# Attention and two MoE layers on one core: the first batch in two query pieces, weights converted 512 columns wide, and moved priorities in the instruction planner

## The chip, the cores and the metric

One Trainium2 chip, one of its NeuronCores. The time is the device time of one execution in microseconds (us). The engines are PE (TensorE; PEld is its weight load), DVE (VectorE), ACT (ScalarE), POOL (GpSimd) and SP (SyncE, which issues nearly all DMAs here).

## The reference

The inputs are q, k, v of shape (4, 8, 576, 64) in float32, a threshold tau, and float64 weights. Three steps follow each other:

```python
scores = scale * np.matmul(q, k.transpose(0, 1, 3, 2))
thresh = np.max(scores, axis=-1, keepdims=True) - tau
scores = np.where(scores >= thresh, scores, -1000000000.0)
attn = softmax(scores);  x = np.matmul(attn, v)         # to (2304, 512)
h = x @ w_in                                            # 512 to 1024
solu = h * softmax(h);  x = (layer_norm(solu) * g_ln) @ w_out
h = x @ w2_in                                           # 512 to 2048
out = (h * np.tanh(softplus(h))) @ w2_out
```

## The kernel before

**How the instructions are ordered.** The kernel does not issue its instructions as the Python code reads. Each step is recorded as a task with an engine, a planned duration, what it depends on, and which buffer slots it takes and uses (`add`). `Plan.run` (L261) then plays the whole list forward: `forward` (L135) gives each engine, whenever it is free, the ready task with the highest key, and returns the order with planned begin and end times; `backward` (L207) plays it from the end and so sets new keys. After 40 turns of this, with six settings each, the order with the shortest planned length is issued. Every engine runs its instructions in that order; so does SP's queue with its DMAs. A slot of a ring of buffers is free for its next taker when the last users are done.

**Attention.** The 32 heads go in 16 pairs, four pairs to each of the four batches. Queries are cut in five tiles: four of 128, and a fifth that holds the last 64 queries of both heads. For each pair `operands` (L593) loads K and Q of both heads (one load of Q each, in two cuts for the first pair) and `load_v` V. For each tile and head `s_tile` (L617) computes a score tile of 128x576 on PE (L640 in the first eight pairs, L649 in the others), takes the row maximum on DVE (L655), the exp on ACT (L656) and the threshold with row sum on DVE (L659): nine score tiles for a pair. For the first four pairs every third tile uses a third score bank, `s3`. `turn` (L669) transposes the result on PE (L684, L687) and copies it out of PSUM on ACT. At the last tile of a pair it also takes the reciprocals of the nine row sums (L677, L678), writes them to a DRAM tensor `rd` and reads them back spread over partitions, in four DMAs. `pv` (L723) multiplies with V (L732), once for the first 256 queries and once for the other 320; after the second, POOL scales all 576 columns (L746) and one DMA writes them to `xd`.

**First MoE.** `x_split` (L761) loads a tile of 128 tokens from `xd`, waiting for all four pairs of the batch, and splits it in a high and a low word (L772, L773). `moe_h` multiplies with W1 (L784), `layer_norm` follows, `moe_t` transposes, and `moe_y` multiplies with W2 (L854).

**Conversions.** `convert` (L474) turns a block of float64 weights of 128 rows by CW = 256 columns into float32: a DMA to `cr`; on ACT the low words (L491) and, for W1 and W2, the absolute high words (L497); on DVE a mask for the second MoE's weights (L494), then clamp (L499), shift (L500) and merge (L502); on POOL the sum (L507 or L509). W1 and W2 then get a high and a low word each (L521, L522). The rings are four slots of `cr` and two each of `cz`, `cl` and `cf`. W1 takes 16 such blocks, W2 16, and the weights of the second MoE 64, 96 in all. The latter are put together in `ws`, seven blocks of a Strassen product with four DVE operations (L555), and go to DRAM as `w2c`.

**Second MoE.** `ff_in` and `ff_out` multiply with the seven products of Strassen's scheme (PE, L948), and fetch the weights from `w2c` with `load_w`. The loop that records the attention's tasks is

```python
for p in range(NH // 2 + 1):
    if p < NH // 2:
        operands(2 * p); operands(2 * p + 1); load_v(p)
    for i in range(QT):
        ...            # s_tile, turn for each head
        if p and i == 0:
            pv(p - 1, 1)
        if p < NH // 2 and i == 2:
            pv(p, 0)
```

Of the kernel before, what the change touches and what calls it, by code (L numbers as in the profile page):

```python
# [8 lines left out]
F32 = mybir.dt.float32  # L9
# [7 lines left out]
TABLES = {n: list(get_activation_tables("")).index(s) for n, s in (("exp", "natural_log_exp_and_others"), ("mish", "mish"))}  # L17

# [40 lines left out]
class Plan:  # L59
# [73 lines left out]
    ORDER = {e: k for k, e in enumerate(("PE", "DVE", "ACT", "POOL", "SP", "-"))}  # L133

# [126 lines left out]
    def run(self):  # L261
# [50 lines left out]
def kernel(  # L312
# [30 lines left out]
    CW = 256  # L343
    PN = 256
    NP = NT // PN
    M0 = 4
    TU = 3 * PN
# [42 lines left out]
    rd = [dram.tile([2 * QT - 1, 128], F32, name=f"rd{i}") for i in range(NH // 2)]  # L390
# [77 lines left out]

    b_cr = buf("cv", "cr", [128, CW, WN], U32 if WN == 2 else F32, 4)
    b_cz = buf("cv", "cz", [128, CW], U32, 2)  # L470
    b_cl = buf("cv", "cl", [128, CW], U32, 2)
    b_cf = buf("cv", "cf", [128, CW], U32, 2)

    def convert(src, r0, c0, put, gain=None, into=None):  # L474
        cr = b_cr.new()
        if into and c0[1] - c0[0] > 128:
            fetch = lambda: D(cr.tile.rearrange("p (i a) b -> p i (a b)", i=2),
                              src[r0:r0 + 128].rearrange("p (i a) -> p i a", i=2)[:, :, c0[0] * WN:(c0[0] + 128) * WN])
        else:
            first = c0[0] if into else c0  # L480
            fetch = lambda: D(cr.tile.rearrange("p a b -> p (a b)"), src[r0:r0 + 128, first * WN:(first + CW) * WN])
        t_f = add("SP", dma(128 * CW * 4 * WN), fetch, new=[cr])
        if WN == 1:
            x, t = lambda: cr.tile[:, :, 0], t_f
            slots = [cr]
        else:
# [17 lines left out]
            if into:  # L504
                at, n, slots, order = into
                wide = lambda x: x.tile.rearrange("p (a b) -> p a b", a=n)
                return add("POOL", gps(CW), lambda: G.tensor_tensor(at(), wide(cf), wide(cl), ALU.add), [t4, t2],  # L507
                           slots if order is None else [], [cl, cf, *slots], order=[order])
            t = add("POOL", gps(CW), lambda: G.tensor_tensor(cf.tile, cf.tile, cl.tile, ALU.add), [t4, t2], use=[cl, cf])  # L509
            slots = [cf]  # L510
        if into:
            at, n, slots, order = into
            return add("DVE", dve(CW), lambda: V.tensor_scalar(f(at()), x().rearrange("p (a b) -> p a b", a=n), 1.0, None, ALU.mult), [t],
                       slots if order is None else [], [cr, *slots], order=[order], port=True)
# [31 lines left out]
    for g in range(NQ):  # L546
        for x, src in enumerate((w2_in, w2_out)):
            WST[x, g] = []
            for k in range(2):
                ws, wh, ts = b_ws.new(), b_wh.new() if x not in RAW else None, []  # L550
                for j in range(2):
                    at = lambda ws=ws, j=j: ws.tile.bitcast(U32)[:, j:7:4 + j]
                    row, cols = ((2 * j + k) * 128, (g * 256, g * 256 + 128)) if x == 0 else ((2 * g + j) * 128, (k * 128, 256 + k * 128))
                    ts.append(convert(src, row, cols, None, into=(at, 2, [ws], ts[0] if ts else None)))
                add7 = lambda o, a, b, op, ws=ws: (dve(128), lambda: V.tensor_tensor(*(f(ws.tile[:, z]) for z in (o, a, b)), op))  # L555
                t = chain("DVE", [add7(3, 4, 6, ALU.add), add7(2, 3, 0, ALU.subtract), add7(5, 1, 2, ALU.subtract), add7(4, 0, 4, ALU.subtract)], ts, use=[ws], port=True)
# [21 lines left out]
    RX, OPS, VL, E, EX, EVT, XST = ({} for _ in range(7))  # L578
# [14 lines left out]
    def operands(n):  # L593
        if n < 2 * R0:
# [3 lines left out]
            for z, c in enumerate((slice(0, 256), slice(256, SP)) if n < 2 else (slice(0, SP),)):  # L598
                w = c.stop - c.start
                q = add("SP", dma(512 * w), lambda c=c: D(f(qh.tile[:, c]), qq[n // H_, n % H_][:, c]), [], [qh] * (z == 0), [qh], order=OPS[n][0][1:])  # L600
                eng, e, cost = (V, "DVE", dve2(w)) if n < 2 else (G, "POOL", 0.16 + w * 0.95e-3)
# [15 lines left out]
    def s_tile(p, i, h):  # L617

        third = p < M0 and (9 * p + 2 * i + h) % 3 == 2
        st, m = (b_s3 if third else b_st).new(), b_m.new()  # L620
        if i == h == 0:
            RX[p] = [b_sr.new()]
# [20 lines left out]
        def go():  # L643
            for c, w in ((0, 256), (256, KW)):
                for y, n in enumerate(heads):
                    _, ks, qh, ql = OPS[n]
# [6 lines left out]
                [t for n in heads for t in OPS[n][0][:2 if p == 0 and i < 2 else None]], [st], slots, mode=int(p < R0))  # L653
# [69 lines left out]
    def pv(p, c):  # L723
# [10 lines left out]
        if c == 0:  # L734
            EVT[p] = [b_xo.new()]
# [425 lines left out]
```

## Time and profile before

| | |
|---|---|
| median of 3 runs | 889.31 us (885.67 to 889.76) |
| profiled execution | 889.64 us, of which the trace spans 887.9 |
| PE, DVE busy | 846.4 and 781.9 us |
| ACT, POOL busy | 617.1 and 338.4 us |
| moved by DMA | 192.6 MB, 217 GB/s over the span |

A profile shows one execution. A group's line gives line, engine and operation, the tiles (out<-in), the count, and behind the bar busy us and mean ns of one, then how long the engine sat idle before it and what ended that. Matmuls are pipelined: one that is shown as 336 ns may follow its forerunner after half of that, so PE can show itself busy at less than its pace. PEclk is the granted clock as a share of full speed.

### The profile page before, as it was taken

The page shows a single profiled execution, that of the slowest core. Times are in us where ns is not written, and L with a number is a line of the kernel's source. Part 1 is how long each engine was busy: PE and PEld are TensorE (multiplying, and loading weights), DVE is VectorE, ACT ScalarE, POOL GpSimd, SP SyncE. Part 2 cuts the span into 40 slices and gives each one's busy share as a digit, 9 for nine tenths or more (in the row PEclk, how much of TensorE's full clock was granted, in tenths as well). Part 3 has the DMA queues.
Part 4 walks back from the last instruction along what each step waited for, and adds up shares of the span by engine and source line. Part 5 has one row for each costly group of instructions (what it writes and reads, how often), then busy time and mean ns, then how long its engine had stood idle before and what let it go on. Part 6 is the DMA issues. An engine that isn't in the chain of part 4 may idle for free.

```text
span 887.9 us, 16722 instructions
## 1 busy us (share of the span) xinstructions
PE 846.4 (95%) x5419; PEld 736.5 (83%) x5419; DVE 781.9 (88%) x1808; ACT 617.1 (70%) x1368; POOL 338.4 (38%) x430
## 2 busy tenths in 40 slices
PE   8898999999999999999999999999999999999997
PEld 4555666777797888887788898999989999999997
DVE  7999889888988999898868899999999997788767
ACT  5888889868888879867555768665756664546432
POOL 2567776666674666444243221112212100010000
PEclk9999999999999999999999999999999999999999
DMA  5545543333746555454997499999999778788541
GB/s 180 187 158 162 170 143 104 121 113 100 228 132 213 166 175 161 130 183 146 324 382 220 143 308 309 386 333 359 328 371 302 250 216 277 231 273 281 191 152 72
DMA packets 154071, 192.62 MB, mean 217 GB/s; under 512 B 15088, under 2 KB 107776, under 8 KB 153984
## 3 DMA queue, kind: packets, MB, share of 16 engines
q1 hardware_dynamic: 153840, 191.55, 66.1%
q8 instruction: 43, 0.70, 0.3%
q14 instruction: 44, 0.36, 0.1%
q10 hardware_dynamic: 144, 0.00, 0.0%
HBM read 140.32 MB, written 51.19 MB: 216 GB/s over the span
## 4 chain that ended last, share of the span: by engine, by line
PE 49%; DVE 19%; ACT 9%; DMA 8%; issue 4%; POOL 3%; SPq 1%; POOLq 0%; DVEq 0%; ACTq 0%
PE hoa L948 21%; PE hob L948 7%; PE p_mo L784 4%; PE p_ta L732 4%; PE p_mo L854 4%; PE p_ta L684 3%; DMA B<-w2c 3%; DVE e L659 3%; PE st L649 2%; DVE m L655 2%; ACT e L656 2%; PE st L640 2%; DVE cf L502 2%; DVE gl L1033 1%; DMA w2c<-ws 1%
## 5 line engine op out<-in xcount | busy, mean ns | idle before, releaser
L948 PE MATMUL hoa<-y,A 128*128 128x384 f32 x648 | 125.7, 336 | 1.1 <-ACT gf L995 1.1
L948 PE MATMUL hoa<-gh,B 128*128 128x384 f32 x484 | 123.5, 336 | 1.2 <-DVE acc L1069 0.9
L659 DVE SCALAR_TENSOR_TENSOR e<-st,m,e 128x576 f32<-128x576 f32 x132 | 106.0, 813 | 15.2 <-ACT e L656 8.0
L948 PEld LDWEIGHTS hoa<-y,A 128*128 128x128 f32 x648 | 112.6, 188 | 2.7 <-ACT gf L995 2.6
L656 ACT ACTIVATE e<-st,m 128x576 f32<-128x576 f32 x132 | 97.0, 744 | 25.7 <-DVE m L655 25.0
L655 DVE TENSOR_REDUCE m<-st 128x1 f32<-128x576 f32 x132 | 97.3, 751 | 17.7 <-PE st L649 9.2
L1005 POOL TENSOR_TENSOR gf<-gf 128x384 f32<-128x384 f32 x24 | 27.6, 1152 | 214.2 <-DVE gf L1005 211.0
L507 POOL TENSOR_TENSOR ws<-cf,cl 128x256 uint32<-128x256 uint32 x64 | 61.1, 964 | 113.7 <-DMA w2c<-ws 59.9
L684 PE MATMUL p_ta<-ident,e 128*128 128x128 f32 x576 | 85.4, 277 | 9.0 <-ACT ey L667 3.0
L1033 DVE TENSOR_TENSOR gl<-gf,gh 128x384 fp32r<-128x384 f32 x168 | 88.9, 567 | 0.7 <-ACT gh L1031 0.7
L948 PEld LDWEIGHTS hoa<-gh,B 128*128 128x128 f32 x484 | 87.0, 188 | 2.8 <-DVE acc L1069 1.9
L684 PEld LDWEIGHTS p_ta<-ident,e 128*128 128x128 f32 x576 | 65.3, 140 | 28.1 <-ACT ey L667 5.9
L854 PE MATMUL p_mo<-LH,W2H 128*128 128x256 f32 x288 | 83.2, 289 | 0.8 <-ACT ys L867 0.8
L948 PE MATMUL hoa<-gl,B 128*128 128x384 f32 x242 | 81.0, 335 | 1.3 <-DVE gl L1033 1.3
L854 PE MATMUL p_mo<-LL,W2H 128*128 128x256 f32 x288 | 81.4, 283 | 0.0
L854 PE MATMUL p_mo<-LH,W2L 128*128 128x256 f32 x288 | 81.4, 283 | 0.0
L1031 ACT ACTIVATE gh<-gf 128x384 fp32r<-128x384 f32 x168 | 77.8, 515 | 0.5 <-DVE gf L1005 0.2
L658 POOL TENSOR_SCALAR m<-m,cs 128x1 f32<-128x1 f32 x144 | 48.4, 339 | 70.8 <-DVE m L655 58.6
L1001 ACT ACTIVATE gf<-gf 128x384 f32<-128x384 f32 x72 | 37.6, 524 | 45.9 <-DVE gf L998 45.3
L1069 DVE TENSOR_TENSOR acc<-acc,hoa 128x384 f32<-128x384 f32 x101 | 54.1, 547 | 14.7 <-PE hoa L948 12.8
L784 PE MATMUL p_mo<-W1H,XH 128*128 128x512 f32 x144 | 60.6, 421 | 2.8 <-DVE LL L839 2.8
L854 PEld LDWEIGHTS p_mo<-LH,W2H 128*128 128x128 f32 x288 | 55.0, 191 | 2.0 <-ACT ys L867 1.1
(127 smaller groups left out, 2299.1 us busy)
## 6 DMA issues: line engine op xcount, KB each, us to landing
A<-w2c SPq DMA_DIRECT2D x140, 256.0 KB, 4.4
y<-yc SPq DMA_DIRECT2D x28, 768.0 KB, 8.6
w2c<-ws SPq DMA_DIRECT2D x32, 448.0 KB, 4.6
B<-w2c SPq DMA_DIRECT2D x112, 128.0 KB, 4.0
cr<-w_in SPq DMA_DIRECT2D x48, 256.0 KB, 3.3
cr<-w_out SPq DMA_DIRECT2D x48, 256.0 KB, 3.5
yc<-yh SPq DMA_DIRECT2D x9, 896.0 KB, 7.0
yc<-ys SPq DMA_DIRECT2D x9, 896.0 KB, 5.3
```

The costliest lines, as they stand in the source:

```text
L507: return add("POOL", gps(CW), lambda: G.tensor_tensor(at(), wide(cf), wide(cl), ALU.add), [t4, t2], slots if order is None else [], [cl, c ...
L655: t = add("DVE", dve(S), lambda: V.tensor_reduce(m.tile[:, 2:3], x(), AX.XY, ALU.max, negate=True), [t], [m], [st])
L656: a = add("ACT", act(S, True) + 0.1, lambda: SC.activation(et(), x(), ACTF.Exp, bias=m.tile[:, 2:3]), [t], [e] if h == 0 else (), [st, m, ...
L658: b = add("POOL", 0.26, lambda: G.tensor_scalar(m.tile[:, 1:2], m.tile[:, 2:3], -1.0, nt8, ALU.mult, ALU.add), [t], use=[m])
L659: t = add("DVE", dve(S) + 0.06, lambda: V.scalar_tensor_tensor(et(), x(), m.tile[:, 1:2], et(), ALU.is_ge, ALU.mult, accum_out=sr.tile[:, ...
L684: TE.transpose(tp.tile[:, k * 128:(k + 1) * 128], e.tile[:, o:o + 128], ident)
L784: TE.matmul(h.tile, l.tile[:, kt], r[:, kt, j * 512:(j + 1) * 512], start=(kt == 0 and x == 0), stop=(kt == KD - 1 and x == 2))
L854: TE.matmul(y.tile[:, :PN], l[:, k, cs], r.tile[:, k], start=(k == 0 and x == 0), stop=(k == KF - 1 and x == 2))
L948: TE.matmul(x.tile[:, :TH], l, r, start=new and n == 0, stop=stop and n == len(steps) - 1, skip_group_check=True)
L1031: a = add("ACT", act(TH), lambda h=h, x=x: SC.activation(h.tile, full(x), ACTF.Copy), [first], [h], [h, x])
L1033: out[c] = h, l, add(e, cost(TH), lambda h=h, l=l, x=x, eng=eng: eng.tensor_tensor(l.tile, full(x), f(h.tile), ALU.subtract), [a, *deps], ...
L1069: d = add("DVE", dve(TH), lambda: V.tensor_tensor(to(), to(), fr(), ALU.add), deps + [CO.get((v, e, i, t))], use=[ac, x])
```

## The change

Three things change. First, the four pairs of the first batch (NS = 4) are recorded in two pieces: all four pairs with their first 256 queries (tiles 0 and 1), then all four with the other 320 (tiles 2 to 4). K, V and the piece's cut of Q are loaded for each piece anew; row sums, `rd`, the scaling and the write to `xd` are made for each piece; `x_split` waits only for the columns that it reads. The third score bank serves the first pieces alone, 5 tiles where it was 12. Second, CW is 512: half as many conversions, with one slot each of `cz`, `cl` and `cf` and two of `cr`. For the second MoE's weights two DMAs fill one `cr`, and the seven blocks of `ws` stand in another order (`SLOT`). Third, `Plan.run` takes the best order's setting and keys, moves the keys of stretches of that order by 568 recorded draws (`moved`), plays forward once more and issues that order.

```diff
+    def moved(self, order):
...
+            middle, half, rare = draw() % len(order), 20 + draw() % 400, 1 + draw() % 5
+            size = (1.0, 3.0, 10.0, 30.0)[draw() % 4]
+            for t in order[max(0, middle - half):middle + half]:
+                if draw() % (1 << rare) == 0:
+                    t.key -= size * (draw() % 2001 - 1000) / 500.0
...
-                    best = length, order, {x: x.bank for x in self.shared}
+                    best = length, order, (wait, avoid), [t.key for t in self.tasks]
             self.backward()
+        for t, t.key in zip(self.tasks, best[3]):
+            pass
+        self.moved(best[1])
+        order = self.forward(*best[2])
+        best = max(t.end for t in order), order, {x: x.bank for x in self.shared}
...
-    CW = 256
+    CW = 512
+    NS = 4
...
-    b_cr = buf("cv", "cr", [128, CW, WN], U32 if WN == 2 else F32, 4)
-    b_cz = buf("cv", "cz", [128, CW], U32, 2)
-    b_cl = buf("cv", "cl", [128, CW], U32, 2)
-    b_cf = buf("cv", "cf", [128, CW], U32, 2)
+    b_cr = buf("cv", "cr", [128, CW, WN], U32 if WN == 2 else F32, 2)
+    b_cz = buf("cv", "cz", [128, CW], U32, 1)
+    b_cl = buf("cv", "cl", [128, CW], U32, 1)
+    b_cf = buf("cv", "cf", [128, CW], U32, 1)
...
-        third = p < M0 and (9 * p + 2 * i + h) % 3 == 2
+        part = p < NS
+        third = p < M0 and ((4 * p + 2 * i + h) % 3 == 2 and i * 128 < C0 if part else (9 * p + 2 * i + h) % 3 == 2)
...
-        if c:
-            *r, rx = RX[p][-5:]
-            ts = [add("POOL", gps(S), lambda: G.tensor_tensor(xo.tile, xo.tile, rx.tile, ALU.mult), EVT[p][1:] + r, use=[xo, rx])]
+        if c or part:
+            if c == 0 or not part:
+                XST[p] = []
+            rx, r = RB[p]
+            o = cs if part else slice(0, S)
+            n = o.stop - o.start
+            t = add("POOL", gps(n), lambda: G.tensor_tensor(xo.tile[:, o], xo.tile[:, o], rx.tile[:, o], ALU.mult), EVT[p][1:] + r, use=[xo, rx])
             k = p % (H_ // 2) * 128
-            XST[p] = add("SP", dma(128 * S * 4), lambda: D(xd[p // (H_ // 2)][k:k + 128, :], xo.tile), ts, use=[xo])
+            XST[p].append((o, add("SP", dma(512 * n), lambda: D(xd[p // (H_ // 2)][k:k + 128, o], xo.tile[:, o]), [t], use=[xo])))
...
-                [XST[p] for p in range(b * H_ // 2, (b + 1) * H_ // 2)], [] if ld else [xr], [xr], ld[:1]))
+                [q for p in range(b * H_ // 2, (b + 1) * H_ // 2) for c, q in XST[p] if c.start < s + l and c.stop > s], [] if ld else [xr], [xr], ld[:1]))
...
-    for p in range(NH // 2 + 1):
-        if p < NH // 2:
-            operands(2 * p)
-            operands(2 * p + 1)
+    todo = []
+    for p, piece in [(p, z) for z in range(2) for p in range(NS)] + [(p, None) for p in range(NS, NH // 2)] + [(None, None)]:
+        if p is not None:
+            operands(2 * p, piece)
+            operands(2 * p + 1, piece)
             load_v(p)
-        for i in range(QT):
+        for i in (range(QT) if piece is None else range(2) if piece == 0 else range(2, QT)):
...
+            while todo:
+                pv(*todo.pop())
+            if p is not None and piece is None and i == 2:
                 pv(p, 0)
+        todo = [(p, piece if piece == 0 else 1)]
```

## Rows read from the trace of the kernel before

**Rows 1.** The page: busy time (part 1); last chain by engine (part 4)

```profile
PE 846.4 (95%) x5419; PEld 736.5 (83%) x5419; DVE 781.9 (88%) x1808; ACT 617.1 (70%) x1368; POOL 338.4 (38%) x430
...
PE 49%; DVE 19%; ACT 9%; DMA 8%; issue 4%; POOL 3%; SPq 1%; POOLq 0%; DVEq 0%; ACTq 0%
```

**Rows 2.** Stages: us; PE, PEld, DVE, ACT, POOL busy (count); PEclk, DMA, GB/s

```profile
0.00:104.00 104.00, 89.09 (x597) 54.46 (x598) 91.34 (x219) 84.81 (x196) 59.40 (x109) 1.00 0.54 172
104.00:440.00 336.00, 325.69 (x2277) 263.94 (x2276) 300.74 (x696) 269.93 (x569) 198.58 (x247) 1.00 0.52 160
440.00:540.00 100.00, 95.42 (x639) 87.85 (x638) 82.28 (x203) 64.39 (x133) 32.67 (x30) 1.00 0.82 267
540.00:888.00 348.00, 336.23 (x1912) 330.28 (x1910) 307.52 (x693) 197.97 (x474) 47.72 (x45) 1.00 0.80 271
```

**Rows 3.** Chain that ended last, in time: start us, us, what

```profile
84.88 5.07 PE p_ta L732 x40
...
494.73 5.72 PE p_mo L784 x24
...
572.30 9.36 PE hoa L948 x54
```

**Rows 4.** Timeline of PE: start us, us, engine, line, operation

```profile
77.04 1.09 PE L684 MATMUL p_ta<-ident,e 128*128 128x128 f32 x8
...
99.49 1.78 PE L640 MATMUL st<-Kst,Qhh 64*128 64x320 f32 x12
```

**Rows 5.** Windows of the first stage's two halves, columns as in 2

```profile
0.00:56.00 56.00, 46.26 (x300) 27.91 (x301) 47.62 (x116) 41.87 (x93) 26.25 (x53) 1.00 0.55 176
56.00:104.00 48.00, 42.83 (x298) 26.55 (x298) 43.72 (x103) 42.94 (x104) 33.14 (x56) 1.00 0.53 167
```

**Rows 6.** Window 56 to 104, PE alone: L640, then L684, then L732

```profile
56.00:104.00 48.00, 16.26 (x96) 1.00 0.53 167
...
56.00:104.00 48.00, 13.05 (x87) 1.00 0.53 167
...
56.00:104.00 48.00, 12.52 (x100) 1.00 0.53 167
```

**Rows 7.** Tile W1H; min/median/max ns, first and last start us

```profile
L784 PE MATMUL p_mo<-W1H,XH x144: 387/395/504, 104.2 to 499.6; 128*128 128x512 f32 x144
...
L522 POOL TENSOR_TENSOR W1L<-cf,W1H x16: 724/732/862, 22.7 to 87.4; 128x256 fp32r<-128x256 f32 x16
```

**Rows 8.** Timeline of POOL and ACT: pair four's scaling, first token tile's split

```profile
92.49 1.41 POOL L746 TENSOR_TENSOR xo<-xo,rx 128x576 f32<-128x576 f32 x1
...
100.27 0.63 ACT L772 ACTIVATE XH<-XR 128x512 fp32r<-128x512 f32 x1
```

**Rows 9.** Tile cr (min/median/max ns), then groups by line (busy us, mean ns)

```profile
L502 DVE SCALAR_TENSOR_TENSOR cf<-cr,cz x96: 355/417/1793, 20.2 to 701.4; 128x256 uint32<-128x256 uint32 x96
...
L499 DVE TENSOR_SCALAR cz<-cz 128x256 f32<-128x256 f32 x96 | 35.7, 379 | 2.2 <-ACT cz L497 2.1
...
L491 ACT ACTIVATE cl<-cr 128x256 uint32<-128x256 uint32 x96 | 41.0, 440 | 13.1 <-POOL ws L507 13.0
...
L507 POOL TENSOR_TENSOR ws<-cf,cl 128x256 uint32<-128x256 uint32 x64 | 61.1, 964 | 113.7 <-DMA w2c<-ws 59.9 <-DVE cf L502 29.4 <-DVE cz L500 6.8
```

**Rows 10.** Groups by line: wider operations of like kind on DVE, ACT, POOL

```profile
L539 DVE TENSOR_TENSOR ws<-ws,wh 128x896 fp32r<-128x896 f32 x16 | 18.2, 1136 | 1.0 <-ACT wh L538 1.0
...
L538 ACT ACTIVATE wh<-ws 128x896 fp32r<-128x896 f32 x16 | 15.2, 949 | 8.8 <-DVE ws L555 8.6 <-DMA B<-w2c 0.2
...
L773 POOL TENSOR_TENSOR XL<-XR,XH 128x512 fp32r<-128x512 f32 x18 | 23.3, 1294 | 24.8 <-ACT XH L772 14.8 <-DMA A<-w2c 6.4 <-ACT ln L810 3.4
```

**Rows 11.** Line L491 on ACT: idle before it (us, times), by ender

```profile
  POOL ws L507: 13.0, 10
```

**Rows 12.** Timeline of PE: the last matmul

```profile
883.62 0.34 PE L948 MATMUL hoa<-gl,B 128*128 128x384 f32 x1
```

**Rows 13.** Window 640 to 720, columns as in 2

```profile
640.00:720.00 80.00, 76.73 (x435) 74.70 (x434) 79.64 (x195) 49.94 (x121) 17.00 (x18) 1.00 0.91 295
```

More of the change, by code (lines that the diff above doesn't have):

```diff
@@ L389 @@
     xd = [dram.tile([DM, S], F32, name=f"xd{i}") for i in range(B)]
[L390 removed]
+    rd = [dram.tile([2 * QT - 1, 128], F32, name=f"rd{i}") for i in range(NH // 2 + NS)]
     P = {"cv": pools(ctx, side="right")("cv")}
@@ L504, in convert @@
             if into:
[L505 to L508, printed above, removed]
+                return add("POOL", gps(CW), lambda: G.tensor_tensor(into[1].tile[:, :4].rearrange("p (a j) n -> p j a n", j=2).bitcast(U32),
+                           *(x.tile.rearrange("p (j a n) -> p j a n", j=2, a=2) for x in (cf, cl)), ALU.add), [t4, t2],
+                           [into[1]], [cl, cf, into[1]])
             t = add("POOL", gps(CW), lambda: G.tensor_tensor(cf.tile, cf.tile, cl.tile, ALU.add), [t4, t2], use=[cl, cf])
@@ L511, in convert @@
         if into:
-            at, n, slots, order = into
-            return add("DVE", dve(CW), lambda: V.tensor_scalar(f(at()), x().rearrange("p (a b) -> p a b", a=n), 1.0, None, ALU.mult), [t],
-                       slots if order is None else [], [cr, *slots], order=[order], port=True)
+            return add("DVE", dve(CW), lambda: V.tensor_scalar(into[1].tile[:, :4].rearrange("p (a j) n -> p j a n", j=2).bitcast(F32),
+                       x().rearrange("p (j a n) -> p j a n", j=2, a=2), 1.0, None, ALU.mult), t_f, [into[1]], [cr, into[1]], port=True)
         if gain is not None:
@@ L549 @@
             for k in range(2):
[L550 to L554, printed above, removed]
+                ws, wh = b_ws.new(), b_wh.new() if x not in RAW else None
+                if x:
+                    part_of = lambda j, src=src, g=g, k=k: src[(2 * g + j) * 128:(2 * g + j + 1) * 128].rearrange(
+                        "p (a b) -> p a b", a=2)[:, :, k * 128 * WN:(k + 1) * 128 * WN]
+                else:
+                    part_of = lambda j, src=src, g=g, k=k: src[(2 * j + k) * 128:(2 * j + k + 1) * 128, g * 256 * WN:(g + 1) * 256 * WN]
+                t = convert(None, (0, 1 - x), None, None, into=(part_of, ws))
                 add7 = lambda o, a, b, op, ws=ws: (dve(128), lambda: V.tensor_tensor(*(f(ws.tile[:, z]) for z in (o, a, b)), op))
-                t = chain("DVE", [add7(3, 4, 6, ALU.add), add7(2, 3, 0, ALU.subtract), add7(5, 1, 2, ALU.subtract), add7(4, 0, 4, ALU.subtract)], ts, use=[ws], port=True)
+                t = chain("DVE", [add7(4, 2, 3, ALU.add), add7(5, 4, 0, ALU.subtract), add7(6, 1, 5, ALU.subtract), add7(2, 0, 2, ALU.subtract)], [t], use=[ws], port=True)
                 if x in RAW:
@@ L577 @@
     b_rx = buf("xs", "rx", [128, S])
-    RX, OPS, VL, E, EX, EVT, XST = ({} for _ in range(7))
+    RB, XST = {}, {}
+    RX, OPS, VL, E, EX, EVT = ({} for _ in range(6))
     EXS, S3 = [], []
@@ L597, in operands @@
             OPS[n] = [t], ks, qh
-            for z, c in enumerate((slice(0, 256), slice(256, SP)) if n < 2 else (slice(0, SP),)):
+            cut = slice(0, C0), slice(C0, SP)
+            for z, c in enumerate(cut if part is None and n < 2 else (slice(0, SP),) if part is None else (cut[part],)):
                 w = c.stop - c.start
                 q = add("SP", dma(512 * w), lambda c=c: D(f(qh.tile[:, c]), qq[n // H_, n % H_][:, c]), [], [qh] * (z == 0), [qh], order=OPS[n][0][1:])
-                eng, e, cost = (V, "DVE", dve2(w)) if n < 2 else (G, "POOL", 0.16 + w * 0.95e-3)
+                eng, e, cost = (V, "DVE", dve2(w)) if n < 2 and not part else (G, "POOL", 0.16 + w * 0.95e-3)
                 OPS[n][0].append(add(e, cost, lambda c=c, eng=eng: eng.tensor_scalar(f(qh.tile[:, c]), f(qh.tile[:, c]), sc, 0.0, ALU.mult, ALU.add),
@@ L673, in turn @@
         deps = done if h == 2 else done[h:h + 1]
-        last = h == 2 and i == KT
-        sums = lambda: sr.tile[:, :2 * KT + 1]
+        part, lo = p < NS, 2 * (p < NS and i * 128 >= C0)
+        last = h == 2 and i == (1 if part and not lo else KT)
+        rows = 2 * (KT - lo) + 1 if i == KT else 4
+        sums = lambda: sr.tile[:, :rows]
         if last:
@@ L688, in go @@
             if last:
-                TE.transpose(tp.tile[:2 * KT + 1, 128:256], sums(), ident)
-        if i == h == 0:
-            for key, b in (((p, 0, 0), b_x[0]), ((p, 0, 1), b_x[0]), ((p, 1), b_x[1]), ((p, 2), b_x[2]), ((p, 3), b_x[3])):
-                EX[key] = [b.new()]
+                TE.transpose(tp.tile[:rows, 128:256], sums(), ident)
+        if i == lo and h == 0:
+            for key, b in (((p, 0, 0), b_x[0]), ((p, 0, 1), b_x[0]), ((p, 2), b_x[2]), ((p, 1), b_x[1]), ((p, 3), b_x[3])):
+                if not part or (lo > 0) == (key[1] % 2 == 1):
+                    EX[key] = [b.new()]
         c = i * 128 >= C0
```

112 lines of the change are left out of this document (73 added, 39 removed).

## The prediction

> **What bounds the kernel now.** I read the engines' shares first, then the stages, then the chain of waits for the pace of PE, and last the operations that the diff touches. The first view shows PE busy 95% of the span and DVE 88%, and the chain that ended last runs 49% through PE, 19% through DVE and 9% through ACT [rows 1]. So no engine is free enough for the whole kernel to be bound by one. The stages tell more [rows 2]. Up to 104 us there is attention alone; PE shows 89.1 us busy (14.9 idle), DVE 91.3 and ACT 84.8. From 104 to 440 attention and the first MoE run mixed, PE idle 10.3 us, DVE 90% busy. From 440 to 540 the first MoE ends (PE idle 4.6), and from 540 there is only the second MoE (PE idle 11.8). The idle sums to 41.6 us. The granted clock is 1.00 in all four stages, so no time is to be had from the clock.
>
> A busy PE is not a PE at its pace. At pace a 384-wide matmul comes every 9.36/54 = 0.173 us, a 512-wide one every 5.72/24 = 0.238, one of L732 every 5.07/40 = 0.127 [rows 3], one of L640 every 1.78/12 = 0.148, a transpose every 1.09/8 = 0.136 [rows 4]. The last stage issues 1912 matmuls; 1912 x 0.173 = 331 of its 348 us. That stage is bound by PE's rate, the diff takes no matmul out of it, and at most 17 us can go there, of which 4.3 are the tail after the last matmul [rows 12]. In the first 104 us it is otherwise. I take the second half of that stage, 56 to 104, where PE shows 42.8 of 48 us [rows 5]: 96 x 0.148 + 87 x 0.136 + 100 x 0.127 = 14.2 + 11.8 + 12.7 = 38.7 [rows 6], and with 13 single transposes of L687 some 40. So 8 us of PE time stand open there, though PE shows only 5.2 idle.
>
> **Part 1, the first batch in two pieces.** Before, the first matmul of the first MoE stands at 104.2, since it needs all of xd of batch 0: the fourth pair's scaling starts at 92.5, and the split of the first token tile at 100.3 [rows 7, 8]. It also needs all of W1; the last W1L starts at 87.4 [rows 7]. After, tokens 0 to 255 need only 16 of the 36 score tiles of the four pairs. If tiles go as evenly as before, the last scaling of the first piece comes at 16/36 x 92.5 = 41 us, and the MoE could start some 12 us later, at 53, as the first matmul now stands 104.2 - 92.5 = 11.7 us behind it. W1 must then be ready 30 us earlier than now. In 0 to 56 DVE is busy 47.6 and ACT 41.9 [rows 5], so room is 8 and 14 us, and half of W1's conversions must fit in. I take a first matmul between 53 and 75 us, 60 as likeliest. Between there and 104 the open time is 8 us of PE, but 4.3 of DVE and 5.1 of ACT [rows 5], and a MoE tile uses all three. Bounds: 0 (it only takes turns with attention) to 8; part 2 frees DVE and ACT just there, so I take 6.
>
> What this adds: each K of the four pairs comes twice (8 more loads), V twice (4), Q in two cuts (6 more), four more writes to xd, four to rd and eight reads back, 34 issues on SP's queue, against 16 fewer for the conversions. The bytes come to 8 x 160 KB + 4 x 320 KB = 2.6 MB more, beside the 172 GB/s x 104 us = 17.9 MB of the stage, whose DMA share is 0.54 [rows 2]: hidden, and if the cover fails each late load holds a score tile by its latency. On DVE come four more pairs of the short operations on sr, under 0.4 us each (nearest: the 0.379 of L499, rows 9), 3 us of DVE, on the path by DVE's share 0.6. On POOL the scaling of the four pairs falls into two, and Q's second cut for heads 0 and 1 moves there from DVE: POOL is 57% busy in that stage [rows 2]. The third score bank now serves 5 tiles instead of 12, so in the second pieces PE waits sooner for a bank; I put 0 to 3 us on it, and take 1, since the MoE can fill such a gap.
>
> **Part 2, conversions 512 wide.** 96 narrow conversions become 48. DVE: the merge L502 has a median of 0.417 at 256 columns, and L539 takes 1.136 at 896 [rows 9, 10]; so a column costs (1.136 - 0.417)/640 = 1.12 ns and a merge of 512 takes 0.704, 0.13 less than two: 48 x 0.13 = 6 us. The clamp L499 takes 0.379 [rows 9]; no wide one is shown, so a pair saves between 0 and 0.379, and I take the middle, 0.19. The shift and, for the second MoE's weights, the mask are of its kind: (48 + 48 + 32) x 0.19 = 24 us, with ends 0 and 48. DVE together 30 us, from 6 to 54. ACT: 0.440 at 256 [rows 9] and 0.949 at 896 [rows 10] give 0.795 ns a column and 0.24 us saved in each of 48 + 16 + 16 pairs: 19 us. POOL: two of 0.964 [rows 9] against one near 1.294 [rows 10], 0.63 each, 20 us; POOL bounds nothing. What lies on the path I take by the shares of the chain: 30 x 0.19 + 19 x 0.09 = 5.7 + 1.7 = 7.4 us (ends 3 and 12). The rest frees engines that were not late. The cost is on the buffers: the same bytes hold one slot of cz, cl and cf instead of two, so ACT's copy of the next low words waits for POOL's add of the last. Today ACT waits for that add 10 times, 13.0 us in all [rows 11].
>
> **Part 3, priorities.** 568 recorded draws move the keys of stretches of the order, and the kernel then keeps the last order; no instruction is added. What they can win is bounded by idle time that the other parts don't touch: 4.6 + 11.8 - 4.3 = 12 us after 440 [rows 2, 12], plus the 10.3 before. Below, an order fitted to planned durations can lose where real ones differ: a loss of 5 is as far as the row goes in which DVE is 79.6 of 80 us busy and PE loses 3.3 [rows 13]. I take a quarter of 22, 5 us.
>
> **Sum.** 6 + 7.4 + 5 - 0.6 - 1 = 17 us off the profiled execution's 889.6 us: 872.6. The median of the runs is 889.3, 0.3 below; the forecast is 872.
>
> **The rivals.**
> *Everything open is filled.* Part 1 wins its 8, part 2 its 12, part 3 half of its 22: 31 us, 858; with some more in the mixed stage 852. For it: 41.6 us of visible idle. Against: DVE saturated from 640 to 720 [rows 13]. 17%.
>
> *DVE and POOL hold each other.* The merge L502 goes up to 1.793 us with a median of 0.417 [rows 9], 1.38 more, about as long as a POOL operation over 512 columns, 1.294 [rows 10]. If half of the 48 wide merges and one other DVE operation beside each meet a POOL operation that is twice as long as now, DVE loses 48 x 1.38 = 66 us of waiting less what it waits today; with half of it new, 33 x 0.19 = 6 us return on the path, and part 1 wins little: 881. The Trainium skill, SBUF — State Buffer, section "SBUF: two separate sides", states that VectorE and GpSimd hold their common port pair for a whole instruction and that the other blocks; by that rule a wider POOL operation is a longer hold, and the maxima of L502 agree. Against: there are half as many holds. 15%.
>
> *The change does not do what it says.* W1 stays late, the MoE starts as before, and the draws gain nothing on real durations: 887 to 889. For it: DVE has 8 us of room up to 56. 7%.
>
> *The one-slot ring stalls ACT.* Where ACT's copy L491 stands in ACT's order ahead of an exp (L656) and POOL's add is late, exp, thresholds and transposes wait too. The price now is 13.0/10 = 1.3 us a wait [rows 11]; with one slot all 48 can wait, 62 us. It decides from the point at which over half of them have an exp behind them: 31 us less some 5 of idle in ACT's cover, 26 on 872: 898. Against: ACT is idle 66 us between 104 and 440 [rows 2], and the order can put the copies late. 7%.
>
> **Chances and range.** The forecast's own case, 863 to 880, has 54%. A measurement of this kernel can tell about 0.5%, 4.4 us, from no change. Faster by more: 54 + 17 + 15 = 86%; within: 7%; slower: 7%. The range reaches down to 855, which leaves out the deeper half of the first rival (8%), and up to 887, which leaves out half of the third and the last (11%): 19% outside.
>
> **What would show it.** The first L784 between 53 and 75 us with all W1L before it: part 1 right; near 104: wrong. L502 48 times at about 0.70 us, ACT's low copy at 0.64, clamps at 0.57: part 2 right. PE idle from 104 to 440 under 8 us and the last stage starting some 13 us earlier: the gain lies before 540, as I say. The last stage shorter than 343 us would mean that the draws did more than I grant. ACT waiting over 40 us for POOL's add in L491 would mean that the ring stalls. Above 887 the forecast is wrong in sign or nearly so, and below 855 in its bounds.

## The result, and the profile after

The changed kernel takes 878.31 us (median of 4 runs, 876.76 to 881.49) against 889.53 (4 runs): a ratio of 0.9873, 95% interval 0.9836 to 0.991. It is 11 us faster, inside the range and on the forecast's side, but 6 us short of the forecast's 872. The profiled execution took 881.49 us, 879.3 of them in the trace. Lines have moved: L640 is now L694, L649 L702, L684 L739, L732 L789, L784 L846, L854 L916, L948 L1012; L491 is L541, L502 L552, L656 L709, L658 L711, L659 L712.

The page's shares of busy time and its last chain by engine, of the changed kernel [before: rows 1]:

```profile
PE 848.3 (96%) x5423; PEld 736.9 (84%) x5423; DVE 766.1 (87%) x1638; ACT 609.4 (69%) x1292; POOL 328.9 (37%) x370
...
PE 69%; DVE 15%; DMA 6%; ACT 4%; issue 3%; POOL 2%; SPq 0%; ACTq 0%; POOLq 0%; DVEq 0%
```

DVE has 15.8 us less to do, and the chain that ended last now runs 69% through PE where it was 49%. The windows by stage (us; PE, PEld, DVE, ACT, POOL busy with counts; PEclk, DMA share, GB/s), and last the half from 56 to 104 [before: rows 2, 5]:

```profile
0.00:104.00 104.00, 95.02 (x606) 58.68 (x606) 91.37 (x197) 85.14 (x173) 64.50 (x100) 1.00 0.65 200
...
104.00:440.00 336.00, 328.75 (x2337) 266.81 (x2336) 293.36 (x631) 268.48 (x544) 189.16 (x218) 1.00 0.54 171
...
440.00:540.00 100.00, 95.79 (x619) 88.58 (x618) 85.41 (x188) 67.78 (x136) 28.09 (x20) 0.98 0.81 263
...
540.00:879.40 339.40, 328.75 (x1868) 322.81 (x1866) 295.95 (x624) 187.97 (x441) 47.13 (x33) 1.00 0.79 267
...
56.00:104.00 48.00, 47.74 (x303) 30.93 (x299) 43.29 (x90) 43.30 (x90) 34.96 (x46) 1.00 0.63 190
```

PE is idle 9.0 us in the first stage instead of 14.9, 7.3 instead of 10.3 in the second, and from 56 to 104 almost never. The last stage has 1868 matmuls left at 540 us instead of 1912: 44 x 0.173 = 7.6 us ahead of the kernel before [rows 2, 3]. The span is 8.6 us shorter, so only 1 us was won after 540. The granted clock is 0.98 from 440 to 540, where it was 1.00.

Tile W1H (min/median/max ns, first and last start in us) shows when the first MoE starts and when W1 is ready [before: rows 7]:

```profile
L846 PE MATMUL p_mo<-W1H,XH x144: 387/397/504, 60.4 to 487.9; 128*128 128x512 f32 x144
...
L570 POOL TENSOR_TENSOR W1L<-cf,W1H x8: 1268/1280/1288, 25.2 to 75.4; 128x512 fp32r<-128x512 f32 x8
```

The first matmul stands at 60.4 us. What PE did up to 104 us, of L694, L739, L789 and L846 in this order, and under it L640, L684 and L732 of the kernel before:

```profile
0.00:104.00 104.00, 32.84 (x188) 1.00 0.65 200
...
0.00:104.00 104.00, 24.16 (x168) 1.00 0.65 200
...
0.00:104.00 104.00, 21.17 (x160) 1.00 0.65 200
...
0.00:104.00 104.00, 14.05 (x48) 1.00 0.65 200
```

```profile
0.00:104.00 104.00, 34.43 (x204) 1.00 0.54 172
...
0.00:104.00 104.00, 26.14 (x174) 1.00 0.54 172
...
0.00:104.00 104.00, 22.88 (x180) 1.00 0.54 172
```

48 matmuls of the first MoE are done early, while 16 of the scores, 6 transposes and 20 of the products with V are put off: 48 x 0.238 - 16 x 0.148 - 6 x 0.136 - 20 x 0.127 = 5.7 us of PE work ahead.

The conversions (tile cr with min/median/max ns, then groups by line with busy us and mean ns) [before: rows 9]:

```profile
L552 DVE SCALAR_TENSOR_TENSOR cf<-cr,cz x48: 675/684/1584, 21.2 to 681.2; 128x512 uint32<-128x512 uint32 x48
...
L549 DVE TENSOR_SCALAR cz<-cz 128x512 f32<-128x512 f32 x48 | 25.4, 529 | 0.7 <-ACT cz L547 0.5
...
L550 DVE TENSOR_SCALAR cz<-cz 128x512 uint32<-128x512 uint32 x48 | 23.0, 479 | 0.1
...
L544 DVE TENSOR_SCALAR cz<-cr 128x512 uint32<-128x512 uint32 x32 | 15.1, 472 | 0.0
...
L541 ACT ACTIVATE cl<-cr 128x512 uint32<-128x512 uint32 x48 | 32.6, 679 | 5.4 <-POOL ws L555 4.6 <-POOL cf L558 0.7
...
L555 POOL TENSOR_TENSOR ws<-cf,cl 128x512 uint32<-128x512 uint32 x32 | 46.3, 1446 | 73.3 <-DMA w2c<-ws 37.5 <-DVE cf L552 11.1 <-ACT acc L1134 7.3
```

A wide merge has a median of 0.684 us, a clamp a mean of 0.529. What a saved instruction is worth on DVE is less than its record, since the records of DVE operations that follow each other overlap, as in the timeline of the kernel before:

```profile
599.52 0.55 DVE L1005 TENSOR_TENSOR gf<-gf 128x384 f32<-128x384 f32 x1
...
599.99 0.54 DVE L1069 TENSOR_TENSOR acc<-acc,hoa 128x384 f32<-128x384 f32 x1
```

The first record ends at 600.07, and the second starts 0.08 us before that.

### The profile page after: what moved, and what is told of

Same layout as the page of the kernel before. It is cut to its first block, busy times and chain, and to the rows that moved or that the text cites. A ratio compares the mean times of both kernels' runs of the same rounds, so it can differ in the third digit from the quotient of the medians.

```text
span 879.3 us, 16385 instructions
## 1 busy us (share of the span) xinstructions
PE 848.3 (96%) x5423; PEld 736.9 (84%) x5423; DVE 766.1 (87%) x1638; ACT 609.4 (69%) x1292; POOL 328.9 (37%) x370
## 4 chain that ended last, share of the span: by engine, by line
PE 69%; DVE 15%; DMA 6%; ACT 4%; issue 3%; POOL 2%; SPq 0%; ACTq 0%; POOLq 0%; DVEq 0%
PE hoa L1012 22%; PE p_mo L846 10%; PE p_mo L916 8%; PE hob L1012 7%; PE p_ta L789 6%; PE p_ta L739 5%; PE st L702 4%; PE st L694 4%; DVE e L712 2%; DVE gl L1100 2%; DVE ws L605 2%; DVE acc L1136 1%; DVE m L708 1%; DMA B<-w2c 1%; PE p_mo L895 1%
## 5 line engine op out<-in xcount | busy, mean ns | idle before, releaser
L1012 PE MATMUL hoa<-y,A 128*128 128x384 f32 x696 | 136.3, 338 | 2.1 <-DMA A<-w2c 1.0
L1072 POOL TENSOR_TENSOR gf<-gf 128x384 f32<-128x384 f32 x24 | 33.9, 1411 | 252.7 <-DVE gf L1072 252.7
L1012 PEld LDWEIGHTS hoa<-y,A 128*128 128x128 f32 x696 | 121.9, 189 | 4.1 <-ACT gf L1062 1.8
L712 DVE SCALAR_TENSOR_TENSOR e<-st,m,e 128x576 f32<-128x576 f32 x139 | 111.2, 812 | 12.9 <-ACT e L709 7.3
L708 DVE TENSOR_REDUCE m<-st 128x1 f32<-128x576 f32 x139 | 102.3, 751 | 19.8 <-PE st L702 10.7
L709 ACT ACTIVATE e<-st,m 128x576 f32<-128x576 f32 x139 | 101.6, 744 | 20.6 <-DVE m L708 19.7
L1012 PE MATMUL hoa<-gh,B 128*128 128x384 f32 x436 | 111.5, 336 | 1.6 <-DVE acc L1136 1.4
L739 PE MATMUL p_ta<-ident,e 128*128 128x128 f32 x576 | 83.7, 277 | 3.5 <-DVE e L712 1.2
L916 PE MATMUL p_mo<-LH,W2H 128*128 128x256 f32 x288 | 83.9, 291 | 0.0
L739 PEld LDWEIGHTS p_ta<-ident,e 128*128 128x128 f32 x576 | 65.1, 140 | 20.9 <-ACT ey L720 3.7
L916 PE MATMUL p_mo<-LL,W2H 128*128 128x256 f32 x288 | 81.4, 283 | 0.0
L916 PE MATMUL p_mo<-LH,W2L 128*128 128x256 f32 x288 | 81.3, 282 | 0.0
L1012 PEld LDWEIGHTS hoa<-gh,B 128*128 128x128 f32 x436 | 78.4, 188 | 3.5 <-DVE acc L1136 2.8
L1012 PE MATMUL hoa<-gl,B 128*128 128x384 f32 x218 | 73.6, 337 | 3.6 <-DVE gl L1100 3.6
L711 POOL TENSOR_SCALAR m<-m,cs 128x1 f32<-128x1 f32 x144 | 51.4, 359 | 64.9 <-DVE m L708 51.0
L555 POOL TENSOR_TENSOR ws<-cf,cl 128x512 uint32<-128x512 uint32 x32 | 46.3, 1446 | 73.3 <-DMA w2c<-ws 37.5
L846 PE MATMUL p_mo<-W1H,XH 128*128 128x512 f32 x144 | 61.3, 426 | 1.8 <-DVE LL L901 1.8
L1012 PE MATMUL hob<-gh,B 128*128 128x384 f32 x236 | 60.6, 338 | 0.4 <-DVE acc L1136 0.4
```

The lines of the kernel that those rows point to most:

```text
L708: t = add("DVE", dve(S), lambda: V.tensor_reduce(m.tile[:, 2:3], x(), AX.XY, ALU.max, negate=True), [t], [m], [st])
L709: a = add("ACT", act(S, True) + 0.1, lambda: SC.activation(et(), x(), ACTF.Exp, bias=m.tile[:, 2:3]), [t], [e] if h == 0 else (), [st, m, ...
L711: b = add("POOL", 0.26, lambda: G.tensor_scalar(m.tile[:, 1:2], m.tile[:, 2:3], -1.0, nt8, ALU.mult, ALU.add), [t], use=[m])
L712: t = add("DVE", dve(S) + 0.06, lambda: V.scalar_tensor_tensor(et(), x(), m.tile[:, 1:2], et(), ALU.is_ge, ALU.mult, accum_out=sr.tile[:, ...
L739: TE.transpose(tp.tile[:, k * 128:(k + 1) * 128], e.tile[:, o:o + 128], ident)
L846: TE.matmul(h.tile, l.tile[:, kt], r[:, kt, j * 512:(j + 1) * 512], start=(kt == 0 and x == 0), stop=(kt == KD - 1 and x == 2))
```

## The experiments

Every kernel was timed beside the kernel before on the same chip. In one table, ratios to the kernel before with 95% intervals:

| pieces | wide | draws | us | ratio |
|---|---|---|---|---|
| yes | yes | 568 recorded (the change) | 878.31 | 0.9873 (0.9836 to 0.991) |
| yes | yes | none | 901.54 | 1.0128 (1.0105 to 1.015) |
| yes | no | none | 897.63 | 1.0076 (1.0054 to 1.0098) |
| no | yes | none | 890.52 | 1.001 (0.9991 to 1.003) |
| no | no | 90 of its own | 886.97 | 0.9969 (0.9945 to 0.9993) |
| no | no | 81 others of its own | 886.84 | 0.9958 (0.9934 to 0.9982) |
| yes | no | 72 of its own | 884.17 | 0.9945 (0.9921 to 0.9968) |
| no | yes | 66 of its own | 885.32 | 0.9952 (0.993 to 0.9975) |
| yes | yes | first 16 recorded | 884.06 | 0.9927 (0.99 to 0.9955) |
| yes | yes | 63 of its own | 879.16 | 0.9868 (0.9837 to 0.9899) |
| yes | yes | 75 others of its own | 876.27 | 0.9847 (0.981 to 0.9883) |
| yes | yes | 568 recorded and 22 more | 874.49 | 0.9811 (0.978 to 0.9843) |
| yes | yes | 568 recorded, PE held twice | 884.3 | 0.993 (0.9903 to 0.9957) |

**One part alone, without draws.** The theory then was the forecast's: three terms that add. The rival: the draws carry the change. The first run takes the draws out:

```diff
-        self.moved(best[1])
-        order = self.forward(*best[2])
-        best = max(t.end for t in order), order, {x: x.bank for x in self.shared}
```

> Pieces and wide conversions stay; the recorded draws are not applied, so the best of the planner's own orders is issued. Theory A (the forecast's terms): the draws are worth 5 us of the 11 measured, so about 883 us (ratio to before 0.992 to 0.995), first MoE matmul near 60 us as in the changed kernel. Theory B (the draws carry the change, because only they let the order use what the other two parts free): 886 to 890 us, ratio 0.996 to 1.002, though the first MoE matmul still comes well before 104 us.

901.5 us: outside both. Without its draws the change makes the kernel slower, by 1.3%, though the first MoE matmul starts at 61.9 us. The second keeps the conversions of the kernel before and the order that the planner finds. Against the changed kernel its edit is, beside the three lines above,

```diff
-    CW = 512
+    CW = 256
...
-    b_cz = buf("cv", "cz", [128, CW], U32, 1)
...
+    b_cz = buf("cv", "cz", [128, CW], U32, 2)
```

> Only the first batch in two pieces; conversions 256 wide with two slots each, no draws. Theory A: the earlier MoE start is worth 6 less 1.6 of additions, about 885 us (ratio 0.993 to 0.997). Theory B: the order does not use it, 888 to 892 us (ratio 0.998 to 1.003). Both: the first MoE matmul later than in the changed kernel, 65 to 80 us, since narrow conversions hold W1 back.

897.6 us, again above both, with the first matmul of the MoE at 74.8, inside the interval. The third has `NS = 0` and `CW = 512`:

> Only the conversions at 512 columns with one slot each; the first batch whole as before, no draws. Theory A: 7 us less, about 882 us (ratio 0.990 to 0.994). Theory B: the time freed on DVE and ACT is not on the path, 887 to 891 us (ratio 0.997 to 1.002). Theory C (the one-slot ring stalls ACT and the draws hide it): 893 us or more, with over 40 us of ACT waiting for POOL's add ahead of the low-word copy. First MoE matmul near 104 us for all.

890.5 us: theory B, no change. Its tile W1H shows the first MoE matmul at 105.1. ACT waits 6.5 us in all ahead of the low-word copy, so theory C falls. The parts don't add: against the forecast's -6 + 1.6 and -7.4 stand +7 and +1 us, and the draws are worth not 5 us but 1.0128 - 0.9873 = 2.55%, 23 us.

**Draws on the other structures.** Do draws win as much anywhere? Each structure got a series (`REFINE`) of its own, kept draw by draw where its planned order grew shorter. For the kernel before that takes the lines of the change, and one order dependence more:

```diff
+        self.moved(best[1])
+        order = self.forward(*best[2])
...
-            a = add("ACT", act(m), lambda c=c: SC.activation(hi.tile[:, c], f(x.tile[:, c]), ACTF.Copy), [t], [] if out else [hi], [hi, x])
+            a = add("ACT", act(m), lambda c=c: SC.activation(hi.tile[:, c], f(x.tile[:, c]), ACTF.Copy), [t], [] if out else [hi], [hi, x], order=[out[0][0]] if out else [])
```

> The kernel before, unchanged in its pieces and conversions, with a series of 90 draws of its own, found in the same way as the recorded one (a draw stays where it shortens the planned order of this kernel); one order dependence is added so that the two halves of a split keep their order. Theory A (the draws carry the gain whatever the structure): 874 to 882 us, ratio to before 0.982 to 0.992, mean granted clock 0.997 or more. Theory B (the draws only repair what pieces and wide conversions spoil, and those two then carry the gain): 886 to 890 us, ratio 0.996 to 1.0. First MoE matmul near 104 us for both.

> The first batch in two pieces, narrow conversions, and 72 draws found for this structure. Theory A: 874 to 882 us, no better than the draws on the kernel before by over 2 us. Theory B: the lead of the early MoE start (5.7 us of PE work at 104 us in the changed kernel) is kept: 4 us or more below the draws on the kernel before.

> Conversions 512 wide with one slot, the first batch whole, and 66 draws found for this structure. Theory A: 876 to 884 us, the same as the draws on the kernel before within 3 us. Theory B: the 15 us less of DVE work come out as time: 4 us or more below the draws on the kernel before.

887.0, 884.2 and 885.3 us. Theory A falls: on the kernel before, draws win 3 us, not 11. On the wide conversions they win 5 us, on the pieces 13 and on both 23, but much of that makes good what the planner's own order had lost. Theory B holds only in part, since neither pieces nor wide conversions alone come 4 us below the first of these kernels (2.8 and 1.7, and the intervals of the ratios overlap). Only both together do. Tile W1H of the draws on the kernel before, and of those on the pieces with narrow conversions:

```profile
L815 PE MATMUL p_mo<-W1H,XH x144: 389/397/504, 99.5 to 494.0; 128*128 128x512 f32 x144
```

```profile
L828 PE MATMUL p_mo<-W1H,XH x144: 387/397/504, 67.5 to 499.0; 128*128 128x512 f32 x144
...
L554 POOL TENSOR_TENSOR W1L<-cf,W1H x16: 725/734/784, 19.8 to 83.2; 128x256 fp32r<-128x256 f32 x16
```

With the batch whole the MoE starts at 99.5, with pieces and narrow conversions at 67.5. The last W1L starts there at 83.2 instead of 75.4, but that is not what holds the first matmul back. The pieces alone without draws have their last W1L at 83.4 as well, and their first matmul at 74.8. What comes later is the split of the first token tile (first the changed kernel, then the pieces with narrow conversions):

```profile
57.79 0.63 ACT L834 ACTIVATE XH<-XR 128x512 fp32r<-128x512 f32 x1
```

```profile
62.80 0.62 ACT L816 ACTIVATE XH<-XR 128x512 fp32r<-128x512 f32 x1
```

**How the draws win.** Only the first 16 of the 568:

```diff
-        for z in range(0, len(REFINE), 4):
+        for z in range(0, 64, 4):
```

> The changed kernel with only the first 16 of its 568 recorded draws. If the draws win by mending a few bad places (PE gaps with a fall of the clock behind them), the first ones do most: 880 to 889 us. If they win by many small shifts all along, 893 to 901 us.

884.1 us: 16 draws bring 17 of the 23 us. Where the time is without draws shows in the windows up to 180 and up to 360 us, first of the kernel without draws, then of the kernel before (columns as above):

```profile
0.00:180.00 180.00, 166.44 (x1094) 108.45 (x1096) 154.55 (x335) 146.83 (x303) 111.06 (x159) 1.00 0.53 166
...
0.00:360.00 360.00, 336.87 (x2329) 249.46 (x2330) 310.67 (x651) 290.23 (x591) 219.25 (x285) 1.00 0.52 159
```

```profile
0.00:180.00 180.00, 164.28 (x1085) 108.17 (x1087) 158.57 (x372) 150.03 (x343) 110.75 (x186) 1.00 0.48 151
...
0.00:360.00 360.00, 339.88 (x2360) 254.90 (x2361) 319.97 (x731) 300.60 (x651) 223.63 (x320) 1.00 0.51 159
```

Without draws PE is 9 instructions ahead at 180 us and 31 behind at 360, of which 18 are 512-wide matmuls of the first MoE (216 against 234). The windows 180 to 360 and 540 to 600 without draws, and under them with 16 (columns as above):

```profile
180.00:360.00 180.00, 170.43 (x1237) 141.01 (x1234) 156.12 (x317) 143.39 (x288) 108.19 (x126) 1.00 0.50 152
...
540.00:600.00 60.00, 55.38 (x297) 53.69 (x296) 54.27 (x111) 39.94 (x96) 8.85 (x7) 0.94 0.96 328
```

```profile
180.00:360.00 180.00, 176.30 (x1290) 147.63 (x1286) 161.78 (x332) 149.84 (x302) 113.31 (x133) 1.00 0.53 164
...
540.00:600.00 60.00, 59.70 (x341) 58.73 (x340) 55.66 (x120) 40.85 (x96) 10.44 (x7) 1.00 1.01 361
```

PE issues 1290 instructions instead of 1237 in the first stretch and 341 instead of 297 in the second. In the first, the threshold operation on DVE waited for POOL's small operation on m, in all and times within this stretch, without draws and with 16:

```profile
  POOL m L706: 7.5, 8
```

```profile
  POOL m L711: 3.5, 9
```

That is 4.0 us less on an engine that is 87% busy, and DVE's busy time there grew by 5.7 us. In the second, the two windows do not show the same part of the work. The wait for gl where the second MoE begins, and the fall of the clock behind it (PEclk 0.94), are not gone with 16 draws; they stand before the window:

```profile
546.15 0.69 PE L1007 MATMUL hoa<-gl,B 128*128 128x384 f32 x1 [2.33 <-DVE gl L1095]
```

```profile
537.22 0.69 PE L1012 MATMUL hoa<-gl,B 128*128 128x384 f32 x1 [2.34 <-DVE gl L1100]
```

So 8.9 of the 15.4 us by which the two traced executions differ (897.5 and 882.1) lie ahead of this place. What wins the rest was not settled, and neither was what the wait for m is worth by itself; both traces are of one execution.

The granted clock, which every run has on record, tells more. Its mean over the runs is 0.991 without draws (5 runs), 0.993 with 16 (4) and 0.998 with all 568 (4). If PE had work all the time, the missing share times the span is what the falls cost: an estimate of 7.7, 6.0 and 2.0 us. By it the clock is under 2 us of what the first 16 draws win, but some 4 of the 5.8 us that the other 552 win.

**Is the recorded series a lucky one?** Two more series on the changed structure, found from nothing; 22 more draws behind the recorded ones; and a second series on the kernel before:

> The changed kernel (pieces and wide conversions) with another series of 63 draws, found from nothing in the same way. Theory A (pieces, wide conversions and any fitted order make the gain together): 875 to 882 us. Theory B (the recorded series is a lucky one, and what an order takes on the chip varies by several us whatever it was fitted to): anywhere from 878 to 890 us, over 3 us from the changed kernel and from the other new series.

> As the run before, with a third series of 75 draws, found with other random numbers. Theory A: 875 to 882 us, within 3 us of the series before. Theory B: over 3 us from it.

> The changed kernel with its 568 draws and 22 more on top, each kept where it shortens the planned order. Theory A: 876 to 879 us, the same or up to 2 us less. Theory B: 876 to 884 us, since small moves late in the search do as much harm as good on the chip.

> The kernel before with a second series of 81 draws found for it. Theory A: 884 to 889 us as with the first series, 6 us or more above the changed kernel: pieces and wide conversions are then worth something that no order of the kernel before gives. Theory B: more than 3 us from the first series; if below 880, the structure is worth nothing.

879.2, 876.3, 874.5 and 886.8 us. Three independent series on the changed structure come to 0.985 to 0.987, two on the kernel before to 0.996 and 0.997: theory A. A fitted order is worth 3 us there and pieces with wide conversions some 8 to 10 us on top, which neither of the two fitted orders of the kernel before gave. Tile W1H of the third series shows the early start again, at 59.2.

The 22 more draws give the fastest kernel of the study: 0.9811 against 0.9873, 1.5 us below theory A's expectation. Its windows 104 to 440 and from 540 on:

```profile
104.00:440.00 336.00, 332.48 (x2374) 271.15 (x2373) 297.13 (x636) 269.30 (x547) 192.02 (x221) 1.00 0.56 176
...
540.00:872.40 332.40, 323.54 (x1834) 316.79 (x1832) 290.50 (x613) 182.83 (x432) 49.37 (x33) 1.00 0.79 268
```

PE is idle 3.5 us from 104 to 440 (7.3 in the changed kernel, 10.3 before), and 1834 matmuls are left at 540, 13.5 us ahead of the kernel before.

**What a PE gap costs.** The changed kernel's timeline of PE where the second MoE begins, and the windows behind the gap (columns as above):

```profile
530.99 0.69 PE L1012 MATMUL hoa<-gl,B 128*128 128x384 f32 x1 [2.53 <-DVE gl L1100]
...
531.48 2.12 PE L1012 MATMUL hoa<-y,A 128*128 128x384 f32 x6
...
534.91 1.22 PE L1012 MATMUL hoa<-y,A 128*128 128x384 f32 x6
```

```profile
530.00:532.00 2.00, 1.01 (x3) 1.01 (x4) 2.00 (x5) 1.94 (x6) 0.06 (x1) 0.75 0.98 313
...
532.00:534.00 2.00, 2.00 (x7) 2.00 (x7) 2.00 (x6) 1.40 (x4) 0.00 (x0) 0.50 1.06 330
...
534.00:536.00 2.00, 2.00 (x12) 2.00 (x12) 1.75 (x5) 1.98 (x6) 0.00 (x0) 0.90 1.01 370
```

After a wait of 2.53 us for DVE's gl the granted clock falls to 0.50 of full speed for some 3.4 us: six matmuls take 2.12 us and three microseconds later 1.22. The traced execution of the kernel before had none of this before its tail. To see whether the gap itself does it, PE was held twice in the second MoE:

```diff
+            for _ in range(hold[1] if hold else 0):
+                SC.activation(hold[0].tile, f(hold[0].tile), ACTF.Copy)
             steps = [(l, r) for a, b in terms for l, r in zip(a(), b())]
...
+            held = {(3, 7): 5, (3, 5): 2}.get((z, g), 0) if c == 0 else 0
```

> The changed kernel with PE held twice late in the second MoE, where it has no other wait: five copies on ACT (about 3 us) of a weight tile onto itself before one matmul, and two copies (about 1.2 us) before another. Theory G (a PE gap of over 2 us costs more than itself, since the granted clock falls behind it): behind the long hold a stretch of some 3.6 us at half the full clock, 384-wide matmuls every 0.32 us or more instead of 0.173, behind the short one none; the time is 3 + 1.7 + 1 = 5 to 6 us above the changed kernel, 882.5 to 885. Theory H (the falls come from elsewhere, such as the switch between the layers): no stretch below full clock behind either hold, 3 to 4.5 us above the changed kernel, 881 to 883.

884.3 us, 6 above the changed kernel's median and 5 by the ratios. The runs go from 879.8 to 886.0, so it is the trace that decides: theory G. PE's timeline at the long hold and at the short one, then the windows behind the long hold, and behind the short one the last:

```profile
735.96 2.25 PE L1014 MATMUL hoa<-y,A 128*128 128x384 f32 x12
...
741.32 3.65 PE L1014 MATMUL hoa<-y,A 128*128 128x384 f32 x12 [3.12 <-ACT A L1011]
...
779.06 1.31 PE L1014 MATMUL hob<-y,A 128*128 128x384 f32 x6 [1.55 <-ACT A L1011]
```

```profile
740.00:742.00 2.00, 0.68 (x4) 0.68 (x5) 0.11 (x1) 1.97 (x4) 0.00 (x0) 1.00 1.09 396
...
742.00:744.00 2.00, 2.00 (x8) 2.00 (x7) 0.38 (x1) 1.42 (x5) 0.00 (x0) 0.50 1.05 392
...
744.00:746.00 2.00, 2.00 (x10) 2.00 (x9) 0.97 (x3) 2.00 (x7) 0.00 (x0) 0.64 0.99 395
...
780.00:782.00 2.00, 2.00 (x14) 2.00 (x13) 0.02 (x1) 0.55 (x2) 0.00 (x0) 1.00 0.99 323
```

Behind 3.12 us of waiting the clock stands at 0.50, and 12 matmuls take 3.65 us where 12 took 2.25 just before, 1.4 more; behind 1.55 us it stays at 1.00. The two waits and the slow matmuls make 3.1 + 1.6 + 1.4 = 6.1 us, and 5 to 6 were measured.

The length of a wait does not decide alone, though. In other traces of this study a fall followed one of 1.72 us (16 draws), while none followed one of 2.21 us (no draws):

```profile
423.61 0.50 PE L846 MATMUL p_mo<-W1H,XH 128*128 128x512 f32 x1 [1.72 <-DVE LL L901]
```

```profile
34.33 0.81 PE L689 MATMUL st<-Kst,Qhh 64*128 64x256 f32 x4 [2.21 <-DVE e L707]
```

PEclk is 0.51 from 424 to 426 us in the first and 1.00 from 32 to 40 in the second. So the bound of 2 us in theory G is not a rule.

## Why the prediction was right, and where its steps failed

The time lies in the range and on the right side. The sum has the right sign and two thirds of the right size, but not for its reasons, and that is partly luck: without draws the other two parts came out at +11 us where the sum gave -6 - 7.4 + 1.6 = -11.8, some 23 worse, and the draws brought 23 where 5 were taken, 18 better. Of the signs named, PE's idle time from 104 to 440 came out (7.3 us, under 8 expected), but the last stage starts 7.6 us ahead and not 13.

*Part 1* is right in its mechanism as long as the order is fitted: the first MoE matmul at 60.4 us (60 was likeliest), 5.7 us of PE work ahead at 104 (6 taken). It is wrong in one condition: not all of W1 has to be there, since the last W1L starts 15 us after the first matmul. And as a term of its own it is wrong in sign: pieces alone cost 7 us in the planner's own order; only where both kernels have draws of their own do they come out 3 us ahead, and there the intervals overlap. Without draws a small lead is there at 180 us (1094 PE instructions against 1085) and gone at 360, as the windows showed. The two small costs in the sum, 0.6 for short operations on DVE and 1 for the third score bank, were not measured alone.

*Part 2* is right in the length of its records: merge 0.684 us (0.70 expected), clamp 0.529 (0.57), low copy 0.679 (0.64). A pair of narrow clamps against one wide saves 2 x 0.379 - 0.529 = 0.23 us (0.19 taken). By count times mean, the merges, clamps, shifts and masks fell from 137 us (means of 0.501, 0.379, 0.337 and 0.319) to 98, 39 where 30 were taken. But DVE's busy time fell by 15.8 us. Part of that is the overlap: 176 conversion instructions fewer, at 0.08 us each, are 14 us that the records count twice. Part is other operations that took longer: the 128 additions on ws rose from a mean of 0.314 us to 0.366 and the 168 products gl from 0.567 to 0.598, 12 us together, while their medians stayed (0.283, and 0.547 and 0.549).

And the step "what lies on the path I take by the shares of the chain" failed: alone the wide conversions gave 890.5 us, no change, where it promised 7.4 us. A share of the chain is not the share of a saving that comes out as time. In part the clock took the saving back: over the 12 runs of that kernel its mean is 0.993, beside 0.998 for the kernel before, by the estimate above some 4 us. The rest was not settled. Together with the pieces W1 is ready 8 us earlier; that this is how they count was not shown.

*Part 3* is the step that failed most: "I take a quarter of 22, 5 us". In this structure the draws are worth 23 us, of which half, 0.0128 x 890 = 11 us, only make good what the other two parts lose without them. Of these 11, some 6 are the clock by the estimate above (7.7 us against 1.9 in the kernel before). Bounding a new order by the idle time of the old kernel left out that the changed kernel's own unfitted order is worse.

*The rivals.* The one-slot ring did not stall ACT: the line of the low-word copy waits for POOL's add

```profile
  POOL ws L555: 4.6, 4
```

4.6 us in four waits, less than the 13.0 before [rows 11]. DVE and POOL holding each other longer is not seen in the merge: its median is 0.684 us and its longest 1.584, 0.90 more, where it was 1.38 more before [rows 9]. The additions on ws and the products gl did get longer, by the 12 us above; whether POOL held them was not shown. The Trainium skill's rule on the common port pair (SBUF — State Buffer, "SBUF: two separate sides") may hold, but no run here shows what it costs. "The change does not do what it says" falls by the 60.4 us. Of "everything open is filled", the run with 22 more draws shows the mixed stage nearly filled (3.5 us idle) and still 874.5, not 858: the last stage, by its windows above, takes 332.4 - 1834 x 0.173 = 15 us more than its matmuls at pace.

*Left open:* why the planner's own orders of the changed structures are slower by 0.8 and 1.3%, beyond the half or so that the clock accounts for by the estimate. For each one order was run, so it isn't known how far unfitted orders of one structure lie apart. And why pieces and wide conversions together give more than their sum of 2.8 and 1.7 us with fitted orders; the earlier W1 and token tile may be part of it, but no run changes those alone.

## What to carry to other kernels

In a kernel that a planner orders, a change of structure and the order found for it are one thing: measure the structure with an order fitted to it, and more than one, or a good change looks like a loss (901.5 against 874.5 to 879.2 us here). An operation that starts earlier or gets cheaper wins only what the order then lets through; look at the PE work done at a few times, not at the shares of engines. And a wait of PE can cost more than its length: here those of 2.5 and 3.1 us cost about half as much again, one of 1.55 us did not. So look at the granted clock of an order's runs as well.

## What the runs showed of the hardware

The granted clock fell behind single waits of PE: 2.53 us in the changed kernel and 3.12 us in the held one were followed by over 3 us at the lower of the two levels (1.2 instead of 2.4 GHz), and so was one of 1.72 us with 16 draws; waits of 1.55 us in the held kernel and of 2.21 us without draws were not. I had written that no time is to be had from the clock; the fall at 531 us costs the changed kernel 2 x (0.25 + 0.50 + 0.10) = 1.7 us of PE at full speed, by the three windows from 530 to 536. Executions of one kernel differ in it too: the draws on the kernel before took 882.37 us at a mean clock of 1.000 and 892.24 at 0.992. And the records of neighbouring DVE operations overlap, by 0.08 us in the lines shown, so the length of a record overstates what a saved instruction gives back.
